# A fused attention and MLP layer on one core: the opening rewritten, loads moved into the head loop, and a split last tile

## The chip, the cores and the metric

The kernel runs on one NeuronCore of a Trainium2 chip. The metric is the device time of one execution in microseconds (us); lower is better. Times are medians over several executions. The profile is of one execution, whose span runs from the first instruction to the last. The engines work side by side and wait for each other through semaphores: TensorE (PE in the profile, with its weight loads as PEld), VectorE (DVE), ScalarE (ACT), GpSimd (POOL) and SyncE (SP), which here only starts transfers.

## The reference

One input x of 2048 tokens by 512 feeds two branches, both through the same layer norm:

```python
xn = _layernorm(x, axis=-1)            # (1, 2048, 512)
q  = (xn @ wq) as 32 heads of 128
k, v = the last 512 rows of 8 cached heads, each used by 4 query heads
p  = softmax(q k^T * 128**-0.5)        # 2048 x 512 for each head
s  = (p @ v, heads side by side) @ wo  # 4096 -> 512
h  = silu(xn @ w1)                     # 512 -> 1792
g  = silu(h @ w2)                      # 1792 -> 512
out = x + s * g
```

All inputs and the output are bfloat16. There is no mask.

## The kernel before

**Tiling.** The 2048 tokens are four blocks (`NBLK`) of 512, and a block is four tiles of 128 tokens (`BLKT`). The contraction over 512 is four chunks (`ND`), the hidden width of 1792 is 14 chunks (`NFC`), and the 512 keys are four chunks (`NKC`). A matmul has 128 x 128 weights and 512 columns nearly everywhere. In all there are 2496 of these: 512 each for the q projection, the scores, the weighted sum and the output projection, and 448 for the two layers of the MLP.

**Stages.** An opening loads x, normalises it and lays it feature-first in `xnT[b]`. For block 0 this goes tile by tile: `stats` (mean and variance, line 96), `rstd_of` (a square root on ACT and a reciprocal on DVE, line 102), `center` (line 108), four transposes on PE (line 293) and a copy on ACT (line 294). Then the whole MLP of block 0 runs (`mlp_units`, line 118): `h_mm` makes one 128-wide chunk of h out of four matmuls, and evacuates it by a tanh on ACT (line 134) and a multiply on DVE (line 135); `o_mm` makes the 512 outputs of one token tile out of 14 matmuls (line 142, evacuated in lines 151 and 152). The statistics of blocks 1 and 2 are scattered over the h chunks. After that the other three blocks are centered into `xnb` and each is turned by one transposing transfer (line 331). Only then the loop over heads starts, after two q projections (`q_proj`, line 174) have been issued.

**The loop.** It takes 128 steps, one for each block and head. Step `s` issues the four score tiles of its head with their exponentials on ACT (`score`, line 187), the normalisation of the probabilities on DVE (`normalise`), the transposing transfer of the previous step's probabilities `p_all` into `pT` (`flip`, line 212), the q projection of step `s + 2`, and the weighted sum of step `s - LAG`, three steps back (`weighted`, line 218). Between the scores, `pump` pops units of independent matmuls from a list `fill`: in the first 32 steps (block 0) the MLP of the blocks 1 to 3, at 10 or 11 units a step, and later, at four a step, the output projection of the block before (`out_units`, line 242). So a step has 22 to 23 matmuls in block 0, and 16 afterwards.

**Buffers.** PSUM has 8 buffers: four for scores (`sc`), one for q, one for the weighted sum, two for the fillers (`f`). `p_all`, `pT` and `qT` have three buffers each. The weights of the MLP and, after them, `wo` share the tags `big0` to `big3`, the hidden values and small tiles the tags `pair0` to `pair6`.

**Order.** The order of work on PE, ACT, DVE and SP is the order of the program text (`manual_schedule`). Each of these engines takes its own instructions strictly in this order, and one that waits holds all behind it. POOL starts the loads of `wo` (line 239), the second loads of x for the residual (line 258) and the stores of the output (line 265); all else goes through SP's queue.

Of the kernel before, what the change touches and what calls it, by code (L numbers as in the profile page):

```python
# [22 lines left out]
def kernel(  # L23
# [62 lines left out]
    def load_x(b):  # L86
        x_blk[b] = work.tile([P, BLKT, D], BF16, name="x_blk", tag="pT", bufs=3)
        if b == 0:
            for j in range(BLKT):
                nc.sync.dma_start(x_blk[b][:, j, :], x2[ds(j * P, P), :])  # L90
        else:
            nc.sync.dma_start(
                x_blk[b], x2[ds(b * BLK, BLK), :].rearrange("(j p) d -> p j d", p=P)
            )

    def stats(b, js, mv):
        for j in js:
            st = work.tile([P, nc.vector.BN_STATS_DIM], FP32, name="st", bufs=4)
            nc.vector.bn_stats(out=st, in_=x_blk[b][:, j, :])  # L99
            nc.vector.bn_aggr(out=mv[:, j, :], in_=st)  # L100

    def rstd_of(mv, js, rstd):
        nc.scalar.activation(
            rstd[:, js[0] : js[-1] + 1], mv[:, js[0] : js[-1] + 1, 1], ACT.Sqrt, bias=eps, scale=1.0
        )
        nc.vector.reciprocal(rstd[:, js[0] : js[-1] + 1], rstd[:, js[0] : js[-1] + 1])

    def center(b, j, mv, rstd, dst):
        nc.vector.tensor_scalar(  # L109
            out=dst,  # L110
            in0=x_blk[b][:, j, :].rearrange("p (c q) -> p c q", q=P),
            scalar1=mv[:, j, 0:1],
            scalar2=rstd[:, j : j + 1],
            op0=ALU.subtract,
            op1=ALU.mult,
        )

    def mlp_units(b, tag):
        units = []
        cur = {}  # L120

        def h_mm(f, c):
            if c == 0:
                cur["ps"] = ps.tile([P, BLK], FP32, name="h_ps", tag=tag, bufs=PS_BUFS[tag])
            nc.tensor.matmul(  # L125
                cur["ps"],
                w1_sb[f // FH][:, c, (f % FH) * P : (f % FH + 1) * P],
                xnT[b][:, c, :],
                start=(c == 0),
                stop=(c == ND - 1),  # L130
            )
            if c == ND - 1:
                th = work.tile([P, BLK], BF16, name="th", bufs=2)
                nc.scalar.activation(th, cur["ps"], ACT.Tanh, scale=0.5)  # L134
                nc.vector.scalar_tensor_tensor(  # L135
                    out=hT[b][f // 2][:, f % 2, :], in0=th, scalar=1.0, in1=cur["ps"], op0=ALU.add, op1=ALU.mult
                )

        def o_mm(j, f):
            if f == 0:  # L140
                cur["ps"] = ps.tile([P, D], FP32, name="oB_ps", tag=tag, bufs=PS_BUFS[tag])
# [14 lines left out]
        units.append(lambda: (new_hT(b), h_mm(0, 0)))  # L156
        for f in range(NFC):
            for c in range(ND):
                if (f, c) != (0, 0):
                    units.append(lambda f=f, c=c: h_mm(f, c))  # L160
        for j in range(BLKT):
            for f in range(NFC):
                units.append(lambda j=j, f=f: o_mm(j, f))
        return units
# [7 lines left out]
    def q_proj(s):  # L172
        b, h = divmod(s, HQ)
        q_ps = ps.tile([P, BLK], FP32, name="q_ps", tag="q", bufs=1)
        hr = h % REP
        for c in range(ND):
            nc.tensor.matmul(  # L177
                q_ps,
                wq_sb[h // REP][:, c, hr * DH : (hr + 1) * DH],
                xnT[b][:, c, :],  # L180
                start=(c == 0),
                stop=(c == ND - 1),
            )
        qT[s] = work.tile([P, BLK], BF16, name="qT", bufs=3)
        nc.vector.tensor_copy(qT[s], q_ps)  # L185
# [32 lines left out]
    def weighted(s):  # L218
        h = s % HQ
        o_ps = ps.tile([P, BLK], FP32, name="o_ps", tag="o", bufs=1)  # L220
        for kc in range(NKC):
            nc.tensor.matmul(  # L222
                o_ps, v_sb[h // REP][:, kc, :], pT[s][:, kc, :], start=(kc == 0), stop=(kc == NKC - 1)
            )
        oT[s] = work.tile([P, BLK], BF16, name="oT", bufs=OT_BUFS)
        nc.vector.tensor_copy(oT[s], o_ps)  # L226
        del pT[s], p_all[s], qT[s], den[s]
# [9 lines left out]
    def load_wo(lo, n, tag):  # L237
        t = reg.tile([P, n, D], BF16, name=f"wo{lo}", tag=tag)
        nc.gpsimd.dma_start(t, A_wo[ds(lo * DH, n * DH), :].rearrange("(h p) n -> p h n", p=P))
        wo_t.append((lo, n, t))  # L240

    def out_units(b):
        units = []
        cur = {}

        def mm(j, h):
            if h == 0:
                cur["ps"] = ps.tile([P, D], FP32, name="s_ps", tag="f", bufs=2)
# [3 lines left out]
                wo_of(h),  # L252
# [3 lines left out]
            if h == HQ // 2:  # L256
                cur["x"] = reg.tile([P, D], BF16, name="x_e", tag=f"pair{4 + j % 2}")
                nc.gpsimd.dma_start(cur["x"], x2[ds((b * BLKT + j) * P, P), :])  # L258
            if h == HQ - 1:
                sg = reg.tile([P, D], FP32, name="sg", tag=f"pair{2 + j % 2}")  # L260
                nc.vector.tensor_tensor(out=sg, in0=cur["ps"], in1=g_sb[b][:, j, :], op=ALU.mult)  # L261
                nc.vector.scalar_tensor_tensor(
                    out=cur["x"], in0=sg, scalar=0.25, in1=cur["x"], op0=ALU.mult, op1=ALU.add
                )
                nc.gpsimd.dma_start(out2[ds((b * BLKT + j) * P, P), :], cur["x"])

        for j in range(BLKT):
            for h in range(HQ):
                units.append(lambda j=j, h=h: mm(j, h))
        return units  # L270

    with tc.manual_schedule(engines={ENG.PE, ENG.Activation, ENG.DVE, ENG.SP}):
        load_x(0)
        w1v = B_w1.rearrange("(c p) f -> p c f", p=P)
        w2v = B_w2.rearrange("(c p) d -> p c d", p=P)
        wqv = A_wq.rearrange("(c p) n -> p c n", p=P)
        for i in range(2):
            nc.sync.dma_start(w1_sb[i], w1v[:, :, i * FH * P : (i + 1) * FH * P])
# [3 lines left out]
        load_x(2)  # L282

        mv0 = work.tile([P, BLKT, nc.vector.BN_AGGR_DIM], FP32, name="mv", bufs=4)
        rs0 = work.tile([P, BLKT], FP32, name="rstd", bufs=4)
        for j in range(BLKT):
            stats(0, [j], mv0)
            rstd_of(mv0, [j], rs0)
            xn = work.tile([P, ND, P], BF16, name="xn", bufs=2)
            center(0, j, mv0, rs0, xn)  # L290
            t_ps = ps.tile([P, ND, P], BF16, name="t_ps", tag="sc", bufs=4)
            for c in range(ND):
                nc.tensor.transpose(t_ps[:, c, :], xn[:, c, :], ident)  # L293
            nc.scalar.copy(xnT[0][:, :, j * P : (j + 1) * P], t_ps)
        load_x(3)
        for g in range(HKV):
            nc.sync.dma_start_transpose(
                kT[g].rearrange("p (o w) -> p o w", o=1), A_k_cache[0, g, ds(SK - W, W), :]
            )
        for g in range(HKV):  # L300
            nc.sync.dma_start(wq_sb[g], wqv[:, :, g * REP * DH : (g + 1) * REP * DH])
            nc.sync.dma_start(
                v_sb[g], A_v_cache[0, g, ds(SK - W, W), :].rearrange("(c p) d -> p c d", p=P)
            )

        u0 = mlp_units(0, "sc")
        NH = NFC * ND
        mvs, rss = {}, {}
        for b in range(1, NBLK):
            mvs[b] = work.tile([P, BLKT, nc.vector.BN_AGGR_DIM], FP32, name="mv", bufs=4)  # L310
            rss[b] = work.tile([P, BLKT], FP32, name="rstd", bufs=4)
        todo = [(b, j) for b in range(1, 3) for j in range(BLKT)]
        for i, u in enumerate(u0):
            if i == NH:
                while todo:
                    b, j = todo.pop(0)
                    stats(b, [j], mvs[b])
                for b in range(1, 3):
                    rstd_of(mvs[b], [0, 1, 2, 3], rss[b])
            u()  # L320
            if i < NH and i % ND == ND - 1 and todo and i // ND >= 2:
                b, j = todo.pop(0)
                stats(b, [j], mvs[b])
        for b in range(1, NBLK):
            if b == 3:
                stats(3, [0, 1, 2, 3], mvs[3])
                rstd_of(mvs[3], [0, 1, 2, 3], rss[3])
            xnb = work.tile([P, ND, BLKT, P], BF16, name="xnb", tag="p_all", bufs=3)
            for j in range(BLKT):
                center(b, j, mvs[b], rss[b], xnb[:, :, j, :])  # L330
            nc.sync.dma_start_transpose(
                xnT[b].rearrange("p c (j q) -> p (c j) q", q=P), xnb[:, :, :, :]
            )

        fill = []
        for b in range(1, NBLK):
            fill += mlp_units(b, "f")
# [10 lines left out]
        q_proj(0)  # L348
        q_proj(1)
        wo_state = 0  # L350
        for s in range(NSTEP):
            b, h = divmod(s, HQ)
            if b >= 1 and h == 0:
                fill += out_units(b - 1)
            if b == 0:
                target = (h + 1) * n_mlp // HQ
                n = target - done
            else:
# [64 lines left out]
```

The softmax here doesn't subtract the row's maximum and nothing guards it: scores larger than these inputs give would overflow.

## Time and profile before

The time is 590.68 us, the median of 6 runs from 589.15 to 592.04 us. The span of the profiled execution is 588.9 us. The table divides it. PE loads counts the weight loads, one for each matmul, and so tells how many matmuls a stretch got through; the next columns are the share of the stretch in which DVE and ACT were busy, the clock granted to TensorE (1 is full) and the mean share in which the 16 DMA engines were busy.

| stretch, us | what runs | PE loads | DVE | ACT | clock | DMA |
|---|---|---|---|---|---|---|
| 0 to 60 | opening, MLP of block 0, first head | 153 | 57% | 42% | 0.91 | 86% |
| 60 to 200 | heads of block 0, MLP of blocks 1 to 3 | 621 | 77% | 71% | 1.00 | 59% |
| 200 to 240 | the end of block 0, `wo` arrives | 168 | 67% | 64% | 1.00 | 87% |
| 240 to 300 | heads of block 1 with the output projection of block 0 | 279 | 85% | 78% | 1.00 | 85% |
| 300 to 500 | blocks 1 to 3 | 927 | 85% | 77% | 1.00 | 84% |
| 500 to 560 | the last heads | 264 | 76% | 66% | 1.00 | 83% |
| 560 to 589 | the last output tiles | 103 | 19% | 0% | 0.96 | 8% |

A stretch in which PE takes its instructions without a gap has the most loads for each microsecond. Where there are fewer, PE waited or ran at the lower clock. The busy time of PE itself says less, since matmuls overlap in the pipeline.

### The profile page before, as it was taken

The page shows a single profiled execution, that of the slowest core. Times are in us where ns is not written, and L with a number is a line of the kernel's source. Part 1 is how long each engine was busy: PE and PEld are TensorE (multiplying, and loading weights), DVE is VectorE, ACT ScalarE, POOL GpSimd, SP SyncE. Part 2 cuts the span into 40 slices and gives each one's busy share as a digit, 9 for nine tenths or more (in the row PEclk, how much of TensorE's full clock was granted, in tenths as well). Part 3 has the DMA queues.
Part 4 walks back from the last instruction along what each step waited for, and adds up shares of the span by engine and source line. Part 5 has one row for each costly group of instructions (what it writes and reads, how often), then busy time and mean ns, then how long its engine had stood idle before and what let it go on. Part 6 is the DMA issues. An engine that isn't in the chain of part 4 may idle for free.

```text
span 588.9 us, 8039 instructions
## 1 busy us (share of the span) xinstructions
PE 546.8 (93%) x2463; PEld 246.0 (42%) x2512; DVE 441.0 (75%) x1184; ACT 390.6 (66%) x1113; POOL 23.8 (4%) x44
## 2 busy tenths in 40 slices
PE   3884899999999997999999999999999999999895
PEld 1331344444444443444444444444444444444342
DVE  3845776787688765888888888888888888888511
ACT  4452776676687666777777777777777777777300
POOL 0000000000000030000000000000000000000010
PEclk9996999999999999999999999999999999999999
DMA  8995356455657779797888888887988797878800
GB/s 287 226 305 110 76 115 106 99 107 109 107 109 168 172 189 205 148 179 143 175 159 171 158 158 171 160 170 147 176 156 167 145 180 149 172 154 172 139 29 24
DMA packets 293018, 89.65 MB, mean 152 GB/s; under 512 B 281968, under 2 KB 290928, under 8 KB 292976
## 3 DMA queue, kind: packets, MB, share of 16 engines
q1 hardware_dynamic: 290320, 80.76, 69.4%
q0 software_dynamic: 2656, 8.39, 5.1%
q8 instruction: 19, 0.31, 0.2%
q14 instruction: 23, 0.19, 0.1%
HBM read 17.30 MB, written 2.10 MB: 33 GB/s over the span
## 4 chain that ended last, share of the span: by engine, by line
issue 58%; PE 27%; DVE 6%; DMA 5%; POOL 2%; ACT 2%; POOLq 0%; DVEq 0%; ACTq 0%
PE oB_ps L142 8%; PE h_ps L125 5%; PE q_ps L177 5%; DMA out_dram<-x_e 4%; PE o_ps L222 4%; PE sc_ps L193 4%; DVE hT L135 2%; POOL x_e L258 1%; DVE st L99 1%; DVE xnb L109 1%; DVE p_all L208 1%; ACT p_all L196 1%; ACT th L134 0%; PE t_ps L293 0%; DVE mv L100 0%
## 5 line engine op out<-in xcount | busy, mean ns | idle before, releaser
L196 ACT ACTIVATE p_all<-sc_ps 128x512 bf16<-128x512 f32 x512 | 305.5, 597 | 116.3 <-PE sc_ps L193 108.7
L193 PE MATMUL sc_ps<-kT,qT 128*128 128x512 bf16 x512 | 193.6, 380 | 0.9
L208 DVE TENSOR_SCALAR p_all<-p_all,rden 128x512 bf16<-128x512 bf16 x512 | 157.9, 351 | 9.1
L249 PE MATMUL s_ps<-wo,oT 128*128 128x512 bf16 x500 | 140.1, 379 | 0.6
L177 PE MATMUL q_ps<-xnT,wq 128*128 128x512 bf16 x499 | 131.6, 383 | 9.7 <-DVE qT L185 9.2
L222 PE MATMUL o_ps<-pT,v 128*128 128x512 bf16 x498 | 129.5, 380 | 6.7 <-DMA pT<-p_all 6.3
L226 DVE CAST oT<-o_ps 128x512 bf16<-128x512 f32 x128 | 88.3, 690 | 48.6 <-PE o_ps L222 46.9
L196 ACT ACTIVATION_READ_ACCUMULATOR p_all<-sc_ps 128x1 f32 x512 | 99.9, 195 | 0.0
L185 DVE CAST qT<-q_ps 128x512 bf16<-128x512 f32 x128 | 88.1, 689 | 8.9 <-PE q_ps L177 8.9
L177 PEld LDWEIGHTS <-wq 128*128 128x128 bf16 x512 | 50.3, 98 | 71.0 <-issue 11.4
L222 PEld LDWEIGHTS <-v 128*128 128x128 bf16 x512 | 49.7, 98 | 67.8 <-DMA pT<-p_all 8.3
L193 PEld LDWEIGHTS <-qT 128*128 128x128 bf16 x512 | 50.2, 98 | 63.8 <-issue 4.2
L249 PEld LDWEIGHTS <-oT 128*128 128x128 bf16 x512 | 50.0, 98 | 60.5
L125 PE MATMUL h_ps<-xnT,w 128*128 128x512 bf16 x219 | 60.7, 393 | 8.1 <-DVE hT L135 7.2
L142 PE MATMUL oB_ps<-w,hT 128*128 128x512 bf16 x219 | 55.8, 379 | 0.5 <-DVE hT L135 0.4
L206 DVE RECIPROCAL rden<-den 128x2 f32<-128x2 f32 x256 | 40.6, 159 | 14.3 <-ACT p_all L196 14.2
L135 DVE SCALAR_TENSOR_TENSOR hT<-th,h_ps 128x512 bf16<-128x512 bf16 x56 | 37.6, 681 | 17.0 <-ACT th L134 16.8
L134 ACT ACTIVATE th<-h_ps 128x512 bf16<-128x512 f32 x56 | 33.1, 597 | 17.4 <-PE h_ps L125 11.2
L125 PEld LDWEIGHTS <-w 128*128 128x128 bf16 x224 | 22.5, 101 | 35.9 <-issue 12.6
L142 PEld LDWEIGHTS <-hT 128*128 128x128 bf16 x224 | 21.9, 98 | 27.0 <-issue 0.7
L261 DVE TENSOR_TENSOR sg<-s_ps,g 128x512 f32<-128x512 f32 x16 | 11.0, 686 | 19.2 <-PE s_ps L249 19.2
L152 DVE SCALAR_TENSOR_TENSOR g<-th,oB_ps 128x512 bf16<-128x512 bf16 x16 | 11.0, 688 | 18.2 <-ACT th L151 18.2
(25 smaller groups left out, 81.2 us busy)
## 6 DMA issues: line engine op xcount, KB each, us to landing
wq<-in_A_wq_dram SPq DMA_DIRECT2D x8, 512.0 KB, 6.5
w<-in_B_w_dram SPq DMA_DIRECT2D x4, 896.0 KB, 9.2
wo<-in_A_wo_dram POOLq DMA_DIRECT2D x4, 896.0 KB, 7.9
pT<-p_all SPq DMA_TRANSPOSE x128, 4.3
x_e<-in_A_x_dram POOLq DMA_DIRECT2D x16, 128.0 KB, 3.3
out_dram<-x_e POOLq DMA_DIRECT2D x16, 128.0 KB, 2.3
x_blk<-in_A_x_dram SPq DMA_DIRECT2D x3, 512.0 KB, 8.7
v<-in_A_v_cache_dram SPq DMA_DIRECT2D x8, 128.0 KB, 6.3
```

The costliest lines, as they stand in the source:

```text
L125: nc.tensor.matmul(cur["ps"], w1_sb[f // FH][:, c, (f % FH) * P : (f % FH + 1) * P], xnT[b][:, c, :], start=(c == 0), stop=(c == ND - 1),)
L135: nc.vector.scalar_tensor_tensor(out=hT[b][f // 2][:, f % 2, :], in0=th, scalar=1.0, in1=cur["ps"], op0=ALU.add, op1=ALU.mult)
L142: nc.tensor.matmul(cur["ps"], hT[b][f // 2][:, f % 2, j * P : (j + 1) * P], w2_sb[f // FH][:, f % FH, :], start=(f == 0), stop=(f == NFC - 1),
L177: nc.tensor.matmul(q_ps, wq_sb[h // REP][:, c, hr * DH : (hr + 1) * DH], xnT[b][:, c, :], start=(c == 0), stop=(c == ND - 1),)
L185: nc.vector.tensor_copy(qT[s], q_ps)
L193: nc.tensor.matmul(sc, qT[s][:, j * P : (j + 1) * P], kT[h // REP], start=True, stop=True)
L196: nc.scalar.activation(p_all[s][:, :, j, :], sc.rearrange("p (kc q) -> p kc q", q=P), ACT.Exp, scale=INV_SQRT_DH, accum_out=den[s][:, j : ...
L206: nc.vector.reciprocal(rden, den[s][:, j0 : j1 + 1])
L208: nc.vector.tensor_scalar_mul(p_all[s][:, :, j, :], p_all[s][:, :, j, :], rden[:, j - j0 : j - j0 + 1])
L222: nc.tensor.matmul(o_ps, v_sb[h // REP][:, kc, :], pT[s][:, kc, :], start=(kc == 0), stop=(kc == NKC - 1))
L226: nc.vector.tensor_copy(oT[s], o_ps)
L249: nc.tensor.matmul(cur["ps"], oT[b * HQ + h][:, j * P : (j + 1) * P], wo_of(h), start=(h == 0), stop=(h == HQ - 1),)
```

## The change

The text of the program is changed in five places.

1. **The opening of block 0.** Statistics are taken for two tiles at a time, with one square root and one reciprocal for the pair. x is centered in place, and PE turns it out of `x_blk` (`turn`, into the PSUM tag `f`), with one of the four copies on ACT and three on DVE (`keep`). PE gets 16 extra matmuls on a tile of zeros (`warm_up`: 11, 2 and 3), whose result nobody reads. The first four chunks of h are made in halves of 256 tokens, first the tokens of tiles 0 and 1, then those of tiles 2 and 3. The first `w1` half arrives in two pieces.
2. **The MLP of block 0.** It cycles over the PSUM tags `sc` and `f` (six buffers instead of four). Statistics of block 1 go between its h chunks, those of blocks 2 and 3 between its output matmuls. Block 1 is centered and turned tile by tile (`flip_x`) early in the output phase, and the first two q projections are put inside that phase, after its matmuls 40 and 49 (counted from 0).
3. **Loads in the loop.** The keys, the q weights and the values of a head group are loaded together (`load_head_group`): groups 0 to 2 before the loop, groups 3 to 7 at the end of the steps 1, 3, 5, 7 and 9. Block 2 is centered and turned in the steps 4 to 7, block 3 in the steps 12 to 15. `x_blk` of blocks 2 and 3 lies in `g_sb`, so these loads need not wait for a buffer of `pT`. The last four pieces of `wo` are started by SP at the ends of the steps 32, 34 and 36.
4. **Interleaving in the first 32 steps.** The q projection and the weighted sum are cut into two pairs of matmuls, and the fillers are dealt out in smaller groups (`cut`). In the later steps, with four fillers, the order of matmuls is as before.
5. **The end.** The last token tile of the output projection is made in two halves of 256 columns, 64 matmuls instead of 32, and the stores of the last block go through SP.

The diff, cut to its core:

```diff
     def load_x(b):
-        x_blk[b] = work.tile([P, BLKT, D], BF16, name="x_blk", tag="pT", bufs=3)
+        x_blk[b] = g_sb[b] if b >= 2 else work.tile([P, BLKT, D], BF16, name="x_blk", tag="pT", bufs=3)
...
+    def flip_x(b, j):
+        nc.sync.dma_start_transpose(xnT[b][:, :, j * P : (j + 1) * P], x_blk[b][:, j, :])
+
+    def load_head_group(g):
+        nc.sync.dma_start_transpose(
+            kT[g].rearrange("p (o w) -> p o w", o=1), A_k_cache[0, g, ds(SK - W, W), :]
+        )
+        nc.sync.dma_start(wq_sb[g], wqv[:, :, g * REP * DH : (g + 1) * REP * DH])
+        nc.sync.dma_start(
+            v_sb[g], A_v_cache[0, g, ds(SK - W, W), :].rearrange("(c p) d -> p c d", p=P)
+        )
...
         for j in range(BLKT):
-            for h in range(HQ):
-                units.append(lambda j=j, h=h: mm(j, h))
+            parts = [(0, D // 2), (D // 2, D // 2)] if last and j == BLKT - 1 else [(0, D)]
+            for lo, n in parts:
+                for h in range(HQ):
+                    units.append(lambda j=j, h=h, lo=lo, n=n: mm(j, h, lo, n))
...
-                nc.gpsimd.dma_start(out2[ds((b * BLKT + j) * P, P), :], cur["x"])
+                (nc.sync if last else nc.gpsimd).dma_start(out2[ds(t * P, P), lo : lo + n], xe)
...
+        stats(0, 0)
+        stats(0, 1)
+        rstd_of(0, 2)
+        center(0, 0)
+        center(0, 1)
+        stats(0, 2)
+        stats(0, 3)
+        warm_up(11)
+        t0 = turn(0)
+        warm_up(2)
+        t1 = turn(1)
+        keep(nc.scalar, t0, 0)
+        keep(nc.vector, t1, 1)
+        warm_up(3)
+        rstd_of(2, 2)
+        center(0, 2)
+        center(0, 3)
...
+        for f in range(NEARLY):
+            for c in range(ND):
+                h_mm(early[f], 0, f, c, 0, HB)
+            if f == 2:
+                t2 = turn(2)
+                t3 = turn(3)
+                keep(nc.vector, t2, 2)
+                keep(nc.vector, t3, 3)
+        for f in range(NEARLY):
+            for c in range(ND):
+                h_mm(early[f], 0, f, c, HB, HB)
+            h_evac(early[f], 0, f)
+
+        hs, os_ = mlp_units(0, lambda i: "f" if i % 3 == 2 else "sc")
+        for i, u in enumerate(hs[NEARLY * ND :]):
             u()
...
+            if c == ND - 1 and f in (5, 7, 9, 11):
+                stats(1, (f - 5) // 2)
+        for i, u in enumerate(os_):
+            u()
+            if i == 2:
+                rstd_of(BLKT, BLKT)
+                for j in range(BLKT):
+                    center(1, j)
+                    flip_x(1, j)
+            if i % 4 == 3 and i // 4 < 2 * BLKT:
+                b, j = divmod(i // 4, BLKT)
+                stats(2 + b, j)
+            if i == 42:
+                rstd_of(2 * BLKT, 2 * BLKT)
+            if i == 40:
+                for q in q_units(0):
+                    q()
+            if i == 49:
+                for q in q_units(1):
+                    q()
+        load_head_group(2)
...
+        wo_plan = {HQ: [(14, 7, "big2")], HQ + 2: [(21, 7, "big3")], HQ + 4: [(28, 2, "pair0"), (30, 2, "pair1")]}
...
+            cut = {4: (0, 0, 0, 0, 2, 2), 10: (2, 2, 2, 1, 1, 2), 11: (2, 2, 2, 1, 2, 2)}[n]
...
+            for u in qu[:2]:
+                u()
+            pump(cut[0])
+            for u in qu[2:]:
+                u()
+            pump(cut[1])
             score(s, 1)
-            if s >= LAG:
-                weighted(s - LAG)
+            for u in pu[:2]:
+                u()
+            pump(cut[2])
+            for u in pu[2:]:
+                u()
+            pump(cut[3])
...
+            if 4 <= s < 8:
+                center(2, s - 4)
+                flip_x(2, s - 4)
+            if 12 <= s < 16:
+                center(3, s - 12)
+                flip_x(3, s - 12)
+            if s % 2 == 1 and 3 + s // 2 < HKV:
+                load_head_group(3 + s // 2)
...
+            for args in wo_plan.get(s, []):
+                load_wo(*args, eng=nc.sync)
```

## The prediction

> **What bounds the kernel now.** I read the slices first, then busy time by stretch, then the waits and the order in time where PE falls short. The slices:
>
> ```profile
> PE   3884899999999997999999999999999999999895
> PEclk9996999999999999999999999999999999999999
> ```
>
> PE is full nearly everywhere except in the first four slices and the last two, and slice 4 (44 to 59 us) ran at a lower clock. By stretch (columns: length, then busy us and count for PE, PEld, DVE, ACT, POOL; clock, DMA share, GB/s):
>
> ```profile
> 300.00:500.00 200.00, 199.06 (x910) 90.57 (x927) 170.57 (x479) 154.58 (x463) 8.33 (x15) 1.00 0.84 161
> 0.00:53.40 53.40, 32.10 (x134) 13.82 (x137) 31.32 (x75) 22.44 (x35) 0.70 (x6) 0.94 0.94 250
> 58.00:80.00 22.00, 19.26 (x86) 8.36 (x87) 17.44 (x44) 17.08 (x48) 0.00 (x0) 1.00 0.45 87
> 200.00:240.00 40.00, 36.21 (x166) 16.16 (x168) 26.93 (x76) 25.42 (x76) 4.51 (x6) 1.00 0.87 186
> 560.00:589.00 29.00, 22.57 (x104) 10.05 (x103) 5.54 (x8) 0.00 (x0) 3.25 (x6) 0.96 0.08 27
> ```
>
> From 300 to 500 us there are 927 weight loads in 200 us, 0.2155 us for each matmul, with no gap: a PE floor. The 2496 matmuls cost 538 us at this rate; the other 51 us of the span are what the change can win. The loss of a stretch is its length less 0.2155 us for each load: 27.3 us from 0 to 53.4 (137 loads, 16 of them short transposes), 5.5 from 53.4 to 80 (98), 3.6 from 80 to 200 (540), 3.8 from 200 to 240 (168), 0.1 from 240 to 500, 3.1 from 500 to 560 (264), 6.7 to the end (103). The opening holds more than half. Its order in time:
>
> ```profile
> 12.53 9.90 PE L125 MATMUL h_ps<-xnT,w 128*128 128x512 bf16 x35 [0.67 <-ACT xnT L294]
> 26.97 1.02 PE L125 MATMUL h_ps<-xnT,w 128*128 128x512 bf16 x4 [0.37 <-DVE hT L135]
> 41.84 1.03 PE L177 MATMUL q_ps<-xnT,wq 128*128 128x512 bf16 x4
> 49.72 1.38 DVE L109 TENSOR_SCALAR xnb<-x_blk,mv,rstd 128x512 bf16<-128x512 bf16 x4
> 51.02 0.68 DVE L185 CAST qT<-q_ps 128x512 bf16<-128x512 f32 x1
> 51.75 0.59 PE L177 MATMUL q_ps<-xnT,wq 128*128 128x512 bf16 x1 [8.88 <-DVE qT L185]
> ```
>
> Four things are to be seen: 12.5 us until the first MLP matmul; h chunks every 1.39 us instead of 0.86, because statistics share DVE with their evacuations; a hole of 8.88 us in which q of head 0 lies behind the centering of three blocks on DVE; and after the hole weight loads 0.43 us apart, twice the steady distance, until the clock returns at 57.4 us.
>
> [...] 0.427 us a matmul from 12.5 to 16.5 us, half clock from 47.2 to 57.4. [...]
>
> **The change, part by part.**
>
> *First matmul.* The first x tile lands at 2.76 us. Two statistics (0.85 us each), square root, reciprocal (0.5 together with hand-overs) and two centers (0.41) put tile 0 at 5.5 us and tile 1 at 5.8. PE's warm-up starts when POOL has filled the zeros, about 2.0 us; 11 matmuls at 0.427 end by 6.0 to 6.7, depending on when the clock rises. Then come transposes, two warm-ups, transposes; the copy of tile 1 stands on DVE behind the statistics of tiles 2 and 3 (to 7.5 us) and ends at about 8.5. The `w1` piece needs 1.05 MB through the queue, which has moved 1.01 MB at 6 to 7 us: here by 7.5. So h starts at 8.5 instead of 12.5, at full clock.
>
> *h.* Half chunks [...] run beside the centers and copies of tiles 2 and 3, which end on DVE at about 11.4. Then 16 half matmuls and 40 full ones would keep PE to 21.8. DVE is slower: from 12.2 us on 14 evacuations at 0.66 and four statistics at 0.73 end at 24.8. PE's first output tile needs the last of them: 25.0, where 24.8 was free.
>
> *Output matmuls of block 0 and q.* PE alone would need 42 more matmuls and 8 for q: 10.8 us. DVE, in program order after 24.8: wait for the square root behind its table load (to 26.4), center of block 1 (1.4), eight statistics (0.8 each, 6.4), two evacuations (1.4), then the cast of q 0: it ends at about 36.2. PE reaches the second q projection at 33.6 and waits 2.6 us, as there is one q buffer. After that it has 4 + 6 matmuls: the first score runs at 38.3 us, where it was at 53.4. The same 120 matmuls lie before it in both, so this is a gain of 15.1 us, less 0.2 for the transposes and 32 half matmuls. A doubt of 3 us on each side is the DVE backlog.
>
> *Clock.* [...] the half-clock stretch after the hole goes: from 53.4 to 57.4 it cost about 2.9 us (11 loads in 4.6 us to 58.0, where 2.4 us would do, and the rest of the step). Gain 2.9[...].
>
> *Interleaving.* From 58 to 80 us 3.2 us were lost, and 3.6 from 80 to 200, where an h chunk waits on its evacuation through two buffers (2.5 us in three waits from 58 to 82). Smaller groups of fillers shorten these waits; but DVE, at 79% there, gets 8 centers more (3.3 us), and the DMA engines get five head groups. A step of block 0 takes 22.5 x 0.2155 = 4.85 us and its flip 2.9 us of DMA time (84% of the steady step of 3.45). A group of 768 KB at 300 GB/s is 2.6 us plus about 0.7 for the keys, every second step: 95% full, over 100% in the steps 4 to 7 with a quarter flip (0.7). Behind a flip are queued on SP the flips that follow, and for a flip waits PE two steps later, and ACT, which needs the `p_all` buffer: some 8.4 us are free and a flip lands in 4.3, so about 4 us of delay are absorbed. I take a gain of 1; bounds: a loss of 5 and a gain of 4.
>
> *wo.* Its pieces arrived at once before, and the flips behind them were late:
>
> ```profile
> ACT p_all L196 <- DMA pT<-p_all: 5.8, 2, 3.6
> PE o_ps L222 <- DMA pT<-p_all: 3.6, 2, 2.5
> ```
>
> The same 2.3 MB now come in three parts, but wholly in steps of 3.45 us in which only 16% of the DMA time is free, and ahead of flips in the same queue. At 300 GB/s they need 7.6 us; about 2.8 come free over five steps, 1 to 2 are absorbed. That leaves 3.3 us lost where 3.8 were: a gain of 0.5, bounds -3 and +3.
>
> *Untouched.* From 240 to 550 us the order of matmuls is the same, and the wait for the last flip (2.1 us) stays.
>
> *The end:*
>
> ```profile
> 581.64 1.03 PE L249 MATMUL s_ps<-wo,oT 128*128 128x512 bf16 x4
> 583.44 0.69 DVE L262 SCALAR_TENSOR_TENSOR x_e<-sg,x_e 128x512 bf16<-128x512 f32 x1
> 584.42 0.55 POOL L265 DMA_DIRECT2D out_dram<-x_e  x1 [6.36 <-DVE x_e L262]
> ```
>
> [...] SP saves POOL's 0.3 us before the store (a load of 128 KB from SP lands in 2.2 us, a store from POOL in 2.3). [...] Gain 0.7, bounds -0.7 and 1.2.
>
> Sum: 14.9 + 2.9 + 1.0 + 0.5 + 0.7 = 20.0 us; 590.7 - 20.0 = 570.7, rounded to 570.5.
>
> **The rivals.**
> 1. *The loop's transfers take back a part.* Head groups and x flips stand ahead of the flips in SP's order, and `wo` too: a loss of 5 in block 0 and of 3 more at `wo` instead of gains of 1 and 0.5, so 580. For it: the 95% above, and the flip waits that the trace already has. Against it: flips have 4 us to spare in block 0. Chance 0.2.
> 2. *The clock falls in the opening.* If the copy of q 0 is later than I think, [...] 3 lost by the longer wait and 3 by the clock, 576. For it: DVE has 16 us of queued work. [...] Chance 0.15.
> 3. *The opening and the interleaving give more*: DVE finishes 2 us earlier and block 0 loses almost nothing, 565. Chance 0.15.
> 4. *Slower than before.* Each of five head groups and three `wo` loads would have to hold PE for 3 us beyond what rival 1 has, 594. Nothing in the profile speaks for stalls that add up so: the hole of 8.88 us alone is worth more than the worst of the bounds for `wo`. Chance 0.03.
>
> **How the numbers follow.** The forecast of 570.5 has 0.47. The range goes from 564, rival 3 with a us below, to 579, which holds rival 2 and the milder half of rival 1. Faster by over 0.3%: all cases but the fourth, with a little left out for what I haven't thought of, 0.95; within 0.3%: 0.02; slower: 0.03.
>
> **What would show it.** The first h matmul near 8.5 us and the first score near 38; one wait of q for its cast of 2 to 3 us in place of 8.88; no half clock after the opening; waits for `pT` no larger than before in block 0, and two or three of 1 to 2 us between steps 33 and 40; last matmul to last store 0.8 us shorter. I am wrong if ACT waits on `pT` repeatedly in the first ten steps, if the half clock returns, or if PE's steady rate of 0.2155 us is lost.

## The result and the profile after

The changed kernel takes 563.95 us (median of 8 runs, 563.01 to 564.62), the kernel before 590.31 (median of 16 runs): a ratio of 0.9551, 95% interval 0.9538 to 0.9563. It is faster, as forecast, but by 26.4 us instead of 20, and lies 0.05 us below the range, on the side of rival 3.

The slices of the changed kernel. PE is at 80% or more in every slice but the last, and no slice shows a lower clock. (The first slice holds the warm-up matmuls, which do no useful work; they start 0.43 us apart, twice the steady distance, and the profile has no record of the clock before 6.9 us.)

```profile
PE   8989999999999998999999999999999999999997
PEclk9999999999999999999999999999999999999999
```

The busy time by stretch, columns as before. From 300 to 500 us there are again 927 weight loads: the floor of 0.2155 us a matmul is untouched. The opening now takes 36.3 us, and its 170 loads are those of the same work as before (120 full matmuls and 16 transposes), 16 warm-ups, 16 more for the half chunks, and the first two of the loop:

```profile
300.00:500.00 200.00, 199.06 (x910) 90.58 (x927) 170.43 (x478) 154.64 (x463) 7.72 (x14) 1.00 0.87 162
0.00:36.30 36.30, 33.38 (x166) 16.40 (x170) 28.77 (x67) 18.22 (x27) 1.16 (x7) 1.00 0.97 239
```

PE's order in time in the opening. The first h matmul starts at 8.1 us (12.5 before), the half chunks and the 40 full matmuls run on without a wait worth naming, q 1 waits 1.0 us for the cast of q 0, and the first score starts at 36.29 us (53.41 before). The last line is the first score of the kernel before:

```profile
1.46 4.87 PE L327 MATMUL warm_ps<-warm 128*128 128x512 bf16 x11 [1.46 <-POOL warm L308]
8.13 1.47 PE L134 MATMUL h_ps<-xnT,w 128*128 128x256 bf16 x12
10.67 10.80 PE L134 MATMUL h_ps<-xnT,w 128*128 128x256 bf16 x55 [0.18 <-DVE xnT L337]
34.14 1.02 PE L195 MATMUL q_ps<-xnT,wq 128*128 128x512 bf16 x4 [1.01 <-DVE qT L204]
36.29 0.38 PE L214 MATMUL sc_ps<-kT,qT 128*128 128x512 bf16 x1
```

```profile
53.41 0.63 PE L193 MATMUL sc_ps<-kT,qT 128*128 128x512 bf16 x1
```

The end: two VectorE operations of 0.42 us, a store from SP (two are merged in the line; the last starts at 558.9 us), and the span ends at 562.2:

```profile
555.42 3.82 SPq L295 DMA_DIRECT2D out_dram<-x_e  x2
558.00 0.42 DVE L291 TENSOR_TENSOR sg<-s_ps,g 128x256 f32<-128x256 f32 x1 [2.61 <-PE s_ps L278]
558.46 0.42 DVE L292 SCALAR_TENSOR_TENSOR x_e<-sg,x_e 128x256 bf16<-128x256 f32 x1
```

Both kernels issue 512 score matmuls, four in each step, so the start of a step's first score is the same point of the program in both. The spans between these points show where the 26.7 us between the two profiled executions come from:

| part, from first score to first score | before, us | after, us | gain | forecast |
|---|---|---|---|---|
| start of the span to step 0 | 53.41 | 36.29 | 17.1 | 14.9 |
| steps 0 to 32 | 162.05 | 155.95 | 6.1 | 2.9 + 1.0 |
| steps 32 to 48 (`wo` arrives) | 59.23 | 58.92 | 0.3 | 0.5 |
| steps 48 to 127 | 271.95 | 271.95 | 0.0 | 0 |
| step 127 to the end of the span | 42.3 | 39.1 | 3.2 | 0.7 |

### The profile page after: what moved, and what is told of

It reads as the page before. It is cut to its first block, busy times and chain, and to the rows that moved or that the text cites. A ratio compares the mean times of both kernels' runs of the same rounds, so it can differ in the third digit from the quotient of the medians.

```text
span 562.2 us, 8174 instructions
## 1 busy us (share of the span) xinstructions
PE 546.7 (97%) x2527; PEld 251.0 (45%) x2576; DVE 440.5 (78%) x1186; ACT 384.3 (68%) x1107; POOL 18.8 (3%) x37
## 4 chain that ended last, share of the span: by engine, by line
PE 85%; DMA 7%; DVE 5%; issue 1%; ACT 1%; POOL 0%; ACTq 0%; SPq 0%; POOLq 0%
PE o_ps L246 18%; PE sc_ps L214 18%; PE s_ps L278 18%; PE q_ps L195 18%; DMA pT<-p_all 7%; PE h_ps L134 6%; PE oB_ps L164 6%; DVE hT L145 2%; DVE st L101 1%; PE warm_ps L327 1%; ACT th L144 1%; DVE mv L102 0%; DVE g L174 0%; DVE p_all L229 0%; DVE qT L204 0%
## 5 line engine op out<-in xcount | busy, mean ns | idle before, releaser
L278 PE MATMUL s_ps<-wo,oT 128*128 128x512 bf16 (+1 forms) x533 | 140.4, 367 | 0.6
L246 PE MATMUL o_ps<-pT,v 128*128 128x512 bf16 x498 | 134.3, 380 | 5.4 <-DMA pT<-p_all 4.9
L195 PE MATMUL q_ps<-xnT,wq 128*128 128x512 bf16 x500 | 134.9, 379 | 1.4 <-DVE qT L204 1.0
L278 PEld LDWEIGHTS <-oT 128*128 128x128 bf16 x544 | 53.2, 98 | 57.6
L134 PE MATMUL h_ps<-xnT,w 128*128 128x512 bf16 (+1 forms) x236 | 64.4, 365 | 1.4 <-DVE hT L145 0.7
L164 PE MATMUL oB_ps<-w,hT 128*128 128x512 bf16 x216 | 62.8, 379 | 0.3
L291 DVE TENSOR_TENSOR sg<-s_ps,g 128x512 f32<-128x512 f32 (+1 forms) x17 | 11.1, 655 | 18.4 <-PE s_ps L278 18.4
```

The source lines that it names most:

```text
L134: nc.tensor.matmul(h_ps[:, lo : lo + n], w1_sb[f // FH][:, c, (f % FH) * P : (f % FH + 1) * P], xnT[b][:, c, lo : lo + n], start=(c == 0), ...
L164: nc.tensor.matmul(cur["ps"], hT[b][f // 2][:, f % 2, j * P : (j + 1) * P], w2_sb[f // FH][:, f % FH, :], start=(f == 0), stop=(f == NFC - 1),
L195: nc.tensor.matmul(cur["ps"], wq_sb[h // REP][:, c, (h % REP) * DH : (h % REP + 1) * DH], xnT[b][:, c, :], start=(c == 0), stop=(c == ND - 1),
L246: nc.tensor.matmul(cur["ps"], v_sb[h // REP][:, kc, :], pT[s][:, kc, :], start=(kc == 0), stop=(kc == NKC - 1))
L278: nc.tensor.matmul(cur["ps"], oT[b * HQ + h][:, j * P : (j + 1) * P], wo_of(h)[:, lo : lo + n], start=(h == 0), stop=(h == HQ - 1),)
```

## The experiments

Each kernel is one edit to the changed kernel or to the kernel before. Its time is a median, with the ratio to the kernel before as it was timed beside it (medians of 590.4 to 591.5 us) and the 95% interval of that ratio; the parts are those of the table above, from the one profiled execution. Where that execution is far from the median, the text says so.

### Undoing parts of the change

**Stores from POOL again.**

```diff
-                (nc.sync if last else nc.gpsimd).dma_start(out2[...
+                nc.gpsimd.dma_start(out2[...
```

> The changed kernel, with the last block's stores started by POOL again; the split of the last tile stays. Theory 1 (what the prediction said): the queue matters only by the 0.3 us before the store starts, so 0.3 to 0.5 us slower than the changed kernel (564.3). Theory 2: the store through SP also ends sooner, with 1.3 to 1.7 us less from the last VectorE operation to the end, so 565.3 to 565.7. The wait for the last transposed probabilities tells nothing of the queue: if it is 2.1 us again with SP still free of stores, it varies by itself.

566.00 us, ratio 0.9588 (0.9572 to 0.9604): 2.0 us above the changed kernel, slightly more than theory 2 had. From step 127 to the end it takes 40.6 us instead of 39.1, which is theory 2's 1.5; the steps 0 to 32, which the edit doesn't touch, were 0.9 us longer in this execution and the steps 32 to 48 0.7 shorter:

```profile
558.58 0.42 DVE L292 SCALAR_TENSOR_TENSOR x_e<-sg,x_e 128x256 bf16<-128x256 f32 x1
559.29 0.54 POOL L295 DMA_DIRECT2D out_dram<-x_e  x1 [2.95 <-DVE x_e L292]
```

From the end of the last VectorE operation (559.00) to the end of the span (563.8) are 4.8 us, as before the change (584.13 to 588.9); through SP they are 3.3. The store waits 0.29 us for POOL, lands 2.3 us after its issue instead of 1.5, and the rest comes after the landing.

**The last tile in one piece.**

```diff
-            parts = [(0, D // 2), (D // 2, D // 2)] if last and j == BLKT - 1 else [(0, D)]
+            parts = [(0, D)]
```

> The changed kernel, with the last token tile in one piece of 512 columns again; stores stay on SP. Theory 1 (the prediction): 0.5 us slower, twice 0.27 us of VectorE time [...]. Theory 2: half the store also lands sooner, 1 us slower or more. [...]

563.62 us, ratio 0.9547 (0.9531 to 0.9562); step 127 to the end 39.2 us, 0.1 more than with the split. The split is worth nothing that the times can tell: it saves 0.54 us of VectorE time, but without it the span ends 3.0 us after the last operation, not 3.3. Two half matmuls take about as long as a whole one: 46 of them took 5.18 us, 0.11 each, and a whole one takes 0.2155.

**The old groups of fillers.**

```diff
-            cut = {4: (0, 0, 0, 0, 2, 2), 10: (2, 2, 2, 1, 1, 2), 11: (2, 2, 2, 1, 2, 2)}[n]
+            cut = {4: (0, 0, 0, 0, 2, 2), 10: (0, 3, 0, 0, 2, 5), 11: (0, 4, 0, 0, 2, 5)}[n]
```

> The changed kernel, with the fillers of the first 32 steps in the groups and places that they had before; all other order stays. Theory 1: the finer groups are what shortened the steps 2 to 32 by 2.7 us and part of the steps 0 to 2, so 2.5 to 3.5 us slower (566.5 to 567.5), with the time in the steps in which h chunks are made. Theory 2: these steps became shorter because the opening leaves them no VectorE backlog and no half clock; then less than 0.7 us slower.

569.64 us, ratio 0.9647 (0.9630 to 0.9663). The steps 0 to 32 take 161.04 us instead of 155.95: the finer groups are worth 5.1 us, more than theory 1 said, and the differences (1.6 in the steps 0 to 2, 0.9 in 2 to 4, 1.1 in 10 to 12, 0.3 in 20 to 24, 1.5 in 24 to 28) are mostly in steps with h chunks. PE's waits for the buffers of h account for it. Over the whole span (busy us, mean ns of one, then idle us before them and what ended it) they come to 5.7 us with the old groups and 0.7 in the changed kernel:

```profile
L134 PE MATMUL h_ps<-xnT,w 128*128 128x512 bf16 x203 | 54.0, 379 | 6.1 <-DVE hT L145 5.7
```

```profile
L134 PE MATMUL h_ps<-xnT,w 128*128 128x512 bf16 x204 | 60.4, 379 | 1.2 <-DVE hT L145 0.7
```

A chunk needs 0.60 us on ACT and 0.68 on DVE before its PSUM buffer is free, and there are two such buffers. Five fillers in a row and three soon after ask for the third chunk before the first is out; groups of one and two don't.

**No warm-up.**

```diff
         def warm_up(n):
-            for _ in range(n):
+            for _ in range(0):
```

> The changed kernel without the 16 extra matmuls on zeros. Theory 1: [...] what it loses reaches the end: 1.5 to 3 us slower (565.5 to 567). Theory 2: VectorE's chain of evacuations and statistics sets the pace from 12 to 34 us and hides the slow clock: less than 0.5 us slower.

565.81 us, ratio 0.9588 (0.9562 to 0.9614): theory 1 (a slow clock at the first h matmuls, whose loss reaches the end), at 1.9 us. The first 12 half matmuls take 2.72 us instead of 1.47, and the first score starts 1.6 us later, at 37.93:

```profile
8.02 2.72 PE L134 MATMUL h_ps<-xnT,w 128*128 128x256 bf16 x12 [1.30 <-ACT rstd L105]
```

**All head groups before the loop.**

```diff
-        load_head_group(2)
+        for g in range(2, HKV):
+            load_head_group(g)
...
-            if s % 2 == 1 and 3 + s // 2 < HKV:
-                load_head_group(3 + s // 2)
```

> The changed kernel, with the head groups 3 to 7 loaded before the loop instead of in the steps 1 to 9. Theory 1 (absorbed): the loads in the loop cost only what shows in the steps 8 to 10, 0.55 us, so 0.5 us faster to 0.5 slower. Theory 2: 3.8 MB ahead of the first flips hold the flips of the steps 0 to 3 back by more than their slack, 2 to 6 us slower. Theory 3: the loads in the loop did cost and taking them out wins over 1 us.

568.59 us, ratio 0.9614 (0.9578 to 0.9651); its times lie between 565.5 and 569.8, and the profiled execution was the shortest, 3 us below the median, so what the others lost beyond it is not seen. In that one the steps 2 to 4 take 11.88 us instead of 9.17 and the steps 8 to 12 take 19.42 instead of 20.42. So theory 2, with a small part of theory 3: spreading the groups over the loop costs about 1 us in the steps 8 to 12 and saves more in front. The wait behind it, from 36 to 62 us (engine, line, what it waited for, us in total, times, longest):

```profile
ACT p_all L217 <- DMA pT<-p_all: 3.0, 1, 3.0
```

**`wo` from POOL, all at once.**

```diff
-            for args in wo_plan.get(s, []):
-                load_wo(*args, eng=nc.sync)
+            if s == HQ - 1:
+                for args in [(14, 7, "big2"), (21, 7, "big3"), (28, 2, "pair0"), (30, 2, "pair1")]:
+                    load_wo(*args)
```

> The changed kernel, with the last four pieces of the output weights started by POOL together at the end of step 31, as before. Theory 1: only the amount counts[...]: within 0.5 us of the changed kernel, the loss only moves from the steps 36 to 40 to the steps 32 to 36. Theory 2: pieces ahead of flips in one queue are worse or better than side by side: over 1 us of difference.

565.25 us, ratio 0.9571 (0.9545 to 0.9597). The steps 32 to 48 take 59.59 us against 58.92: a loss of 4.3 over the floor of 55.25 instead of 3.7, earlier and in one stall. By the median, 1.3 us above the changed kernel, it is theory 2; the profiled execution, at 564.20 the shortest of the four, shows 0.7 us here. So the amount counts most, and the placing is worth 0.7 to 1.3 us. PE waits 2.5 us at once (1.7 at most in the changed kernel), and the clock falls to 0.50 after it, which three pieces apart avoid (1.00 from 195 to 235 us in the changed kernel):

```profile
200.00:204.00 4.00, 1.82 (x7) 0.79 (x8) 0.92 (x3) 1.53 (x5) 0.00 (x0) 0.88 1.14 209
204.00:206.00 2.00, 2.00 (x6) 0.68 (x5) 0.92 (x5) 1.11 (x4) 0.00 (x0) 0.50 1.07 200
```

**q after the output matmuls.**

```diff
-            if i == 40:
-                for q in q_units(0):
-                    q()
-            if i == 49:
-                for q in q_units(1):
-                    q()
         load_head_group(2)
+        for s in range(2):
+            for q in q_units(s):
+                q()
```

> The changed kernel, with the first two q projections after the output matmuls of block 0 instead of among them. Theory 1: VectorE's order is what counts; with the cast behind all of its statistics and the last evacuation, q 1 waits for the cast of q 0 by 1.5 to 2.5 us, and the first score is 1 to 2 us later (565 to 566). Theory 2: the place in the order does not matter as long as centering is out of the way: within 0.3 us.

567.03 us, ratio 0.9601 (0.9574 to 0.9629). The first score is 1.5 us later, as theory 1 said, but the steps 0 to 2 take 1.8 us more, so the time lies 1 us above theory 1's range. PE's wait of 2.7 us, and then the clock from 39 to 41 us:

```profile
36.91 1.02 PE L195 MATMUL q_ps<-xnT,wq 128*128 128x512 bf16 x4 [2.71 <-DVE qT L204]
```

```profile
37.00:39.00 2.00, 1.43 (x6) 0.50 (x6) 0.69 (x1) 0.69 (x2) 0.00 (x0) 0.93 0.00 0
39.00:41.00 2.00, 2.00 (x6) 0.73 (x5) 0.00 (x0) 0.00 (x0) 0.00 (x0) 0.50 0.00 0
41.00:43.00 2.00, 2.00 (x9) 0.73 (x7) 0.74 (x2) 0.68 (x2) 0.00 (x0) 0.71 0.00 0
```

Here half clock followed a wait of 2.71 us. The prediction had a wait of 2.6 us and no half clock after it; that was the author's estimate, which no run had shown, and it wasn't safe to assume.

### One part alone, on the kernel before

**The kernel before, again.**

> The kernel before, once more, to see what of its profile repeats. If the 2.7 us for which the last weighted sums waited for transposed probabilities belong to its text, they come again within 0.3 us. If they vary by themselves, they lie between 1 and 2.7, as the runs of the changed kernel and its variants do (1.1 to 2.2). The half clock after the hole should come again.

589.23 us in one execution, span 587.1. The wait at the end is 2.3 us, 0.4 below the first time, so a little outside what was set for it, but above all of the changed kernel's (1.1 to 2.2). The hole (8.89 us) and the half clock (10.2 us of it) come again. The first score is at 52.65 us, so the 17.1 of the table above is 16.4 to 17.1.

**q ahead of the centering.**

```diff
+        q_proj(0)
+        q_proj(1)
         for b in range(1, NBLK):
             if b == 3:
...
-        q_proj(0)
-        q_proj(1)
         wo_state = 0
```

> The kernel before, with one part of the change: the first two q projections are issued ahead of the centering of blocks 1 to 3. Theory 1: this fills the hole of 8.88 us only for eight matmuls and the first scores; the MLP of block 1 then waits for its transposed input, which is as late as before, so 1 to 4 us faster (586 to 589), with the wait at the first h matmul of the loop instead of at q. Theory 2: the order of the cast alone made the hole: 8 to 11 us faster (579 to 582).

587.33 us, ratio 0.9930 (0.9905 to 0.9956): theory 1. The first score is at 45.63 us, 7 to 8 us earlier, and the steps 0 to 32 take 4.5 to 4.9 us longer. The hole has moved to the first h matmul of the loop, which waits for the transposed input of block 1:

```profile
52.43 1.44 PE L125 MATMUL h_ps<-xnT,w 128*128 128x512 bf16 x3 [4.84 <-DMA xnT<-xnb]
```

So the place of the cast alone did not make the hole. It had to be filled by work that is ready, which is what the changed kernel does by centering and turning block 1 under the output matmuls.

**Last stores from SP.**

```diff
-                nc.gpsimd.dma_start(out2[...
+                (nc.sync if b == NBLK - 1 else nc.gpsimd).dma_start(out2[...
```

> The kernel before, with one part of the change: the stores of the last block go through SP. Theory 1: 1.3 to 1.7 us faster (588.6 to 589.0), as the changed kernel loses when they go back to POOL. Theory 2: within 0.5 us, the loss there had another cause.

588.87 us, ratio 0.9965 (0.9948 to 0.9981). Step 127 to the end takes 40.2 us instead of 41.9 to 42.3, and from the last VectorE operation to the end are 3.0 us instead of 4.8. Theory 1, from the other side: 1.8 us.

**`wo` from SP, in three parts.**

```diff
+        wo_plan = {HQ: [(14, 7, "big2")], HQ + 2: [(21, 7, "big3")], HQ + 4: [(28, 2, "pair0"), (30, 2, "pair1")]}
...
-            if wo_state == 1 and done >= n_mlp:
-                load_wo(14, 7, "big2")
...
+            for args in wo_plan.get(s, []):
+                load_wo(*args, eng=nc.sync)
```

> The kernel before, with one part of the change: the last four pieces of the output weights are started by SP at the ends of the steps 32, 34 and 36. Theory 1: where these loads start sets how late the last transposed probabilities come; the wait at the end falls from 2.3 to 2.7 us to 1.1 to 1.4, and the kernel is about 1 us faster. Theory 2: it stays above 2.2 us, the cause is another, and the time stays within 1 us. In the steps 32 to 40 the loss stays at 3.4 to 4 us in both.

589.59 us, ratio 0.9985 (0.9973 to 0.9997). The wait at the end stays at 2.4 us: theory 2. The loss over the floor in the steps 32 to 48 is 3.1 us (3.7 and 4.0 in the two executions of the kernel before).

**The new groups of fillers.** The q projection and the weighted sum are cut into units as in the changed kernel.

```diff
-            if s + 2 < NSTEP:
-                q_proj(s + 2)
-            pump(n - n // 2 - n // 4 if n > 4 else 0)
+            for u in qu[:2]:
+                u()
+            pump(cut[0])
+            for u in qu[2:]:
+                u()
+            pump(cut[1])
             score(s, 1)
...
```

> The kernel before, with one part of the change: fillers, q projections and weighted sums of the loop in the new groups and places. Theory 1: the parts add, the steps 2 to 32 become 2.5 to 3.5 us shorter and the steps 0 to 2 up to 1.6: 3 to 5 us faster (585.5 to 587.5). Theory 2: the new fillers pay only after the new opening, with VectorE free of its backlog: under 1.5 us faster, or slower, since the first h matmul then stands before the second score and waits for the transposed input of block 1.

586.31 us, ratio 0.9937 (0.9906 to 0.9968). The steps 0 to 32 take 156.5 us instead of 161.7 to 162.1, a gain of 5.2 to 5.6, and PE's waits for the buffers of h fall from 7.2 us over the whole span to 2.1. By the times the gain is 3.7 us (1.9 to 5.6), with the profiled execution 1.2 us below the median of six. This is theory 1, by the times inside its range and by the steps above it: the fillers pay without the rest of the change, too.

### Going on

**q earlier.** In the changed kernel:

```diff
-            if i == 42:
+            if i == 33:
                 rstd_of(2 * BLKT, 2 * BLKT)
-            if i == 40:
+            if i == 16:
...
-            if i == 49:
+            if i == 34:
```

> The changed kernel, with the first two q projections after the output matmuls 16 and 34, and the last square root after 33 instead of 42. Theory 1: the wait of q for its cast, 1.0 us, vanishes, and the table load between the last tanh and the first exponential (1.3 us on ScalarE) goes to where nobody waits: 1 to 2 us faster (562 to 563). Theory 2: the backlog on VectorE only moves and holds the first steps: within 0.5 us.

562.49 us, ratio 0.9518 (0.9497 to 0.9539). The first score is at 35.62 us, 0.7 earlier, and the steps 0 to 2 take 0.6 us less: 1.3 of theory 1. The wait of q falls from 1.0 to 0.5 us:

```profile
30.23 1.02 PE L195 MATMUL q_ps<-xnT,wq 128*128 128x512 bf16 x4 [0.48 <-DVE qT L204]
```

**Transfers spread further**, on top of it. Head groups at other steps, two heads of `wo` in each of the steps 32 to 40, and another order for block 0:

```diff
+        GROUP_AT = {1: 3, 8: 4, 10: 5, 16: 6, 18: 7}
...
+            if HQ <= s <= HQ + 8:
+                for h in (14 + 2 * (s - HQ), 15 + 2 * (s - HQ)):
...
+                    nc.sync.dma_start(wo_of(h), A_wo[ds(h * DH, DH), :])
...
+        if b == 0:
+            order = [(j, h) for lo, hi in ((0, 14), (14, HQ)) for j in (0, 1) for h in range(lo, hi)]
+            order += [(j, h) for j in (2, 3) for h in range(HQ)]
+            return [lambda j=j, h=h: mm(j, h, 0, D) for j, h in order]
```

> The changed kernel with the early q projections, and with transfers spread further: the head groups 3 to 7 in the steps 1, 8, 10, 16 and 18; the last 18 heads of the output weights two in each of the steps 32 to 40; and the output projection of block 0 does heads 0 to 13 of two token tiles before it needs head 14. Theory 1: what the steps 32 to 40 lose (3.7 us) is DMA work that does not fit beside the flips; at 0.9 us a step against 0.55 free, with some delay absorbed, 0.5 to 1.5 us stay, and the steps 4 to 16 lose under 0.5: 559 to 560.5. Theory 2: what counts is the total, and the loss stays near 3.7: 562 to 562.5.

561.59 us, ratio 0.9497 (0.9473 to 0.9522), below the changed kernel and, within the intervals, level with q earlier; the time lies between the ranges of the two theories. The steps 4 to 12 lie on the floor, where the changed kernel had lost 1.0 us and the kernel with q earlier 0.1, so spreading the groups gains no more than executions differ by. For `wo` theory 2 holds: the steps 32 to 38 lose nothing any more, and the steps 38 to 48 lose 3.4 us, so the loss came later and stayed.

## Why the forecast gain was too small

Between the profiled executions the gain is 26.7 us where 20.0 were forecast. Of the 6.7 us that are missing, 2.2 lie in front of the loop, 2.2 in the steps 0 to 32 (over 3 too little for the interleaving, over 1 too much for the clock) and 2.5 at the end; `wo` gave 0.2 less than forecast.

**What bounds the kernel:** right. The floor is unchanged, and all gains are places where PE fell short of it.

**First matmul and h:** right. h was forecast for 8.5 us and came at 8.1; the last evacuation for 24.8, and it ended at 24.0. (The terms given for it, 12.2 + 14 x 0.66 + 4 x 0.73, come to 24.4.)

**Output matmuls and q:** the mechanism was right, DVE's backlog holding the cast of q 0, but a term was too large: "wait for the square root behind its table load (to 26.4)". The table load did not follow the evacuations, it ran beside the last two, since ACT's tanh is two chunks ahead of DVE. The lines are from the changed kernel:

```profile
22.72 1.28 ACT L105 ACT_TABLE_LOAD   x1
22.75 1.25 DVE L145 SCALAR_TENSOR_TENSOR hT<-th,h_ps 128x512 bf16<-128x512 bf16 x2
24.02 0.30 ACT L105 ACTIVATE rstd<-mv,eps 128x4 f32<-128x4 f32 x1
24.35 0.18 DVE L108 RECIPROCAL rstd<-rstd 128x4 f32<-128x4 f32 x1 [0.34 <-ACT rstd L105]
33.43 0.66 DVE L204 CAST qT<-q_ps 128x512 bf16<-128x512 f32 x1
```

DVE went on at 24.5 us, 1.9 us earlier than forecast: 0.8 because the last evacuation ended earlier, 1.1 because the wait for the square root took 0.5 us instead of 1.6. The 9.6 us of work after that were forecast as 9.8. The cast ended at 34.1 instead of 36.2, and the first score came at 36.3 instead of 38.3; with the 0.2 that the forecast had taken off, this is 2.2 us of the missing gain.

**Clock: "Gain 2.9".** Too large. Between kernels with the same fillers the steps 0 to 4 became 1.4 to 1.8 us shorter (22.1 to 22.5 us before, 20.7 with the old groups in the changed kernel; 19.9 with the new groups in the kernel before, 18.2 in the changed one). This is all that the new opening, the clock among it, is seen to do for the loop. How much the clock alone is worth was not measured apart.

**Interleaving: "I take a gain of 1; bounds: a loss of 5 and a gain of 4".** This is the step that failed worst. The new groups are worth 5.1 us, by undoing them, to 5.6, by adding them to the kernel before (5.7 and 3.7 by the times). Against this stands what the added transfers and centers cost in the steps 8 to 16: 0.7 to 1.1 us in these executions, 0.4 to 2.0 in all with the new groups and the loads in the loop. So the term was worth 4.1 to 4.5, just beyond its upper bound. From 58 to 200 us 6.8 us were lost in the kernel before, and I took 1 of them because of the transfers and the DVE work that move into the loop. These were mostly absorbed: even the steps 4 to 8, where the prediction had the DMA engines over 100% full, lie on the floor. And from 53.4 to 58 us I gave the whole loss to the clock, while 1.5 to 1.9 us of the steps 0 to 2 were the fillers'.

**`wo`:** right, 0.3 where 0.5 was forecast, though executions differ by more. However its last 18 heads were started, at once or in three or nine parts, from POOL or from SP, the steps 32 to 48 lay 2.9 to 4.0 us over the floor, and 4.2 to 4.7 in the three executions where the clock fell there.

**The end: "Gain 0.7".** It was 3.2. The store through SP saves 1.5 to 1.8 and not 0.3: the forecast priced the 0.3 us before the issue alone. The landing also comes 0.3 to 0.7 us sooner after the issue, and the span ends 0.5 to 1.2 us sooner after the landing. In all, the runs have 4.8 to 4.9 us from the last operation to the end through POOL and 2.7 to 3.3 through SP. The other 0.4 of the forecast stood for the split, as the author's estimate, and the split was worth 0.1: the last two VectorE operations took 0.42 us each at 256 columns (0.69 at 512), but the span ended 3.3 us after them instead of 3.0.

The other part, 1.2 to 1.6 us, is the wait for the last `pT`, which the forecast left at 2.1 us. Its total from the last head on, in the kernel before and in the changed one:

```profile
PE o_ps L222 <- DMA pT<-p_all: 2.7, 2, 2.1
```

```profile
PE o_ps L246 <- DMA pT<-p_all: 1.1, 2, 0.7
```

The kernel before and its four variants have 2.3 to 2.7 us, the changed kernel and its nine variants 1.1 to 2.2. The queue of the stores, the queue of `wo` and the fillers were each changed alone on the kernel before, and none of them brings it out of this range. The cause stays open, but the traces have a lead. The last flip is issued 5.0 us after the first score of step 127 in every run. In the kernel before and its variants the profile then has a packet of 16 KB of the kind `instruction` on the DMA engines while the flip is under way, and the flip lands 5.3 to 5.8 us after its issue. In eight of the ten runs with the text of the changed kernel it has no such packet there, and the flip lands after 4.4 to 4.5 us. In the other two it has one (16 KB without the warm-up, 8 KB with `wo` from POOL at once), and the flip takes 5.1 and 5.3 us; these are the two with the longest waits, 1.9 and 2.2 us. The lines are from the stretch of the last flip, in the kernel before and in the changed one, which has no line of the kind:

```profile
q8 instruction: 1, 0.02, 1.0%
pT<-p_all SPq DMA_TRANSPOSE x1, 5.8
```

```profile
pT<-p_all SPq DMA_TRANSPOSE x1, 4.5
```

No run moves this packet by itself, so that it delays the flip is not shown.

**The rivals.** Rival 3 was nearest, and for its reasons as far as they go: the cast was done 2.1 us earlier, and the loss in the steps 0 to 32 fell from 9.5 us to 3.4 (708 matmuls at 0.2155 us make 152.6). The 2.5 us at the end are in no rival. Rival 2 did not come about: the wait was 1.0 us; with 2.71 us (q after the output matmuls) the clock fell to 0.50. Rival 1's stalls did come where all head groups were loaded at once.

## What to carry to other kernels

Price a filler's place in the order as carefully as its work: what a PE stream loses to buffers that are not yet free can be read from the floor (here 0.2155 us a matmul), and dealing the fillers out in ones and twos took PE's waits for the buffers of h from 5.7 us to 0.7. Moving an instruction ahead of a queue fills a hole only if what follows it is ready as well: on the kernel before, with q ahead of the centering, the first h matmul waited 4.84 us. And price the end of a kernel from the last operation to the end of the span, for the queue that carries the last store (here 4.8 to 4.9 us through POOL, 2.7 to 3.3 through SP).

## What the runs showed of the hardware

- Half clock after waits of 2.3 to 2.8 us: it followed waits of PE of 2.34 us (new groups on the kernel before), 2.47 (`wo` from POOL at once), 2.71 (q after the output matmuls) and 2.79 (last stores from SP on the kernel before), began 0.2 to 1.8 us after PE had started again, and lasted 3.4 us each time. After a wait of 2.54 us in the kernel before the clock stayed at 1.00 (215 to 240 us), and no wait of 2.17 us or less in the loop brought half clock.
- With the last store from POOL the span ended 4.8 to 4.9 us after the last VectorE operation, with one from SP 2.7 to 3.3, for 64 and for 128 KB.
- Half matmuls of 256 columns, each with its own weights, ran 0.11 us apart (46 in 5.18 us), with the weight loads, 98 ns each, beside them.
- A copy of 128 x 512 from PSUM to SBUF took DVE 0.42 us for bfloat16 (line 337), and 0.69 for fp32 (line 204).
